# Mask selections ahead of GpSimd's loads, another layout for k and q of two pairs, another order of the front, and one set of loads less

## The chip, the cores and the metric

The kernel runs on one core of a Trainium2 chip. The metric is the device time of one execution in microseconds. TensorE (PE) multiplies matrices, VectorE (DVE) and ScalarE (ACT) work elementwise, GpSimd (POOL) makes masks and zeroes and also issues some DMAs, and SyncE (SP) issues the others.

## The reference

Four batches of 8 heads, 576 positions, head dimension 64, all in float32. Attention first, in two parts that are added; then two gated feed-forward blocks, the first on the attention's output, the second on the first's.

```python
def attention(q, k, v):
    # pooled part: means of 4 neighbouring positions, softmax over 144, repeated 4 times
    q_d, k_d, v_d = (t.reshape(B, H, S // 4, 4, D).mean(axis=3) for t in (q, k, v))
    out_up = np.repeat(sm_attn(q_d, k_d, v_d), 4, axis=2)
    # local part: only keys with |i - j| < 4
    scores = scale * np.matmul(q, k.transpose(0, 1, 3, 2))
    scores = np.where(mask, scores, -1e9)
    return out_up + softmax(scores) @ v

def moe(x, w_in, conv_w, w_out):        # 512 -> 1024 -> 512
    h = np.maximum(x @ w_in, 0.0)
    gate = sigmoid(conv over 3 positions of h, one filter per channel)
    return (h * gate) @ w_out

def moe2(x, w_val, conv_w, w_out):      # 512 -> 512 -> 512
    gate = sigmoid(causal conv over 5 positions of x)
    return (gate * (x @ w_val)) @ w_out
```

## The kernel before

**Units of work.** A step `s` is one pair of heads of one batch: pairs 0 to 3 are batch 0, pair 4 is the first of batch 1, 16 in all. For each pair: k and q are loaded with positions on partitions and transposed on PE (`tpk`, `tpq`, in `transp`), evacuated by ACT (`kT`, `qT`, in `evac`), pooled by DVE (`kd`, `qd`); v is pooled (`pv`). The local part works on 24 blocks of 24 queries against 32 keys: `sl` adds the mask by a matmul of identity and `maskr` and then the scores, `mxl`, `sub`, `xl`, `sml`, `mul` are the softmax, `tr` transposes, `avl` and `avm` multiply with the windows of v (tile `ldw`), `xn` and `xo` add the pooled part. The pooled part is `sd`, `mxd`, `xd`, `smd`, `scd`, `etd`, `etc`, `avd`, `od`. The pair's output is split into two numbers of lower precision (`xhi`, `xlo`) for the first feed-forward block, whose matmuls run as three products of high and low parts.

**Weights.** They come as raw 64-bit words; each block of 128 x 512 is converted and split by `Weights.pieces`: `ab` (ACT), `cv` (four DVE instructions), `hi` (ACT), `lo` (one DVE instruction). There are 8 blocks for w_in and 8 for w_out (two for each of the four column blocks of the second matmul).

**The front.** Batch 0's attention is written out by hand as the list `FRONT`: names of steps with the pair's number, issued in that order on PE, DVE and ACT, each engine in order (`ordered`). The first four w_in splits (`ab0` to `lo3`) and the convolution weights (`cwa0` to `cwc0`) are in it too. Ahead of it, SP is handed the loads in this order: k and q of pairs 0 and 1, v of the first four heads, half of the windows of v (12 gathers), k and q of pair 2, the rest of v, k and q of pair 3, four blocks of w_in, the convolution weights, and v, k, q of pair 4. POOL makes the identity, zeroes the two tiles `h`, makes `mask` (a zeroing and 12 selections, two for each of six regions) and issues the other 12 gathers; in which order these stand on POOL is left to the scheduler. In batch 0, k and q lie with a partition's six positions of one head side by side (`[QT, 2, NT, D]`), and each transpose takes 12 matmuls; in later batches the two heads lie side by side (`[QT, NT, 2, D]`), and it takes 6 in transpose mode. Each matmul of the 12 is two records in the profile.

**The rest.** From pair 4 on each pair takes eight slots, and between slots PE gets units of the feed-forward block of the batch before: 16 units of the first matmul (`a_mm`, two for each of 8 column blocks, behind each pair of which DVE runs the convolution over 3 positions and the gate) and 16 of the second (`b_mm`, four for each of 4 column blocks). `due_at(slot)` tells how many units must have been issued by a slot. In batch 0 a unit whose index is in `SPLITS` also splits a weight block and loads a further one; the first four of them are w_in's, the other eight w_out's. `next_load` and `next_v` load k, q, v of the pair after; they also ran at pair 3 and so loaded pair 4's again, which had been loaded ahead of the stream.

Of the kernel before, what the change touches and what calls it, by code (L numbers as in the profile page):

```python
# [8 lines left out]
F32 = mybir.dt.float32  # L9
# [54 lines left out]
def kernel(  # L64
# [13 lines left out]
    nc = tc.nc  # L78
    B, H, S, D = q.shape
# [4 lines left out]
    HP = H // 2  # L84
    SD = S // 4
    HD = SD // 2
    QT = 96
    NT = S // QT
# [14 lines left out]
    NSTEP = B * HP  # L103
# [3 lines left out]
    mp = ctx.enter_context(tc.tile_pool(name="mp", bufs=1))  # L107
# [5 lines left out]
    mask = const.tile([128, MW], F32, name="mask")  # L113
# [6 lines left out]
    HT = [mp.tile([128, S + 2], F32, name=f"h{i}") for i in range(2)]  # L120
    turn = {"n": 0, "both": True}

    def pair(name):

        turn["n"] += 1
        pool = psm if turn["both"] and turn["n"] % 2 else psd
        return pool.tile([128, 2, 512], F32, tag="pair", name=name)
# [6 lines left out]
    def key_start(j):  # L134

        return min(max(QB * j - 4, 0), S - KB)
# [3 lines left out]
    def mm(*a, **kw):  # L140
        last["pe"] = nc.tensor.matmul(*a, **kw)  # L141
# [12 lines left out]
            return call  # L154

    vec, act = Noted(nc.vector, "vec"), Noted(nc.scalar, "act")

    def ordered(fn, engines=("pe",)):

        with ExitStack() as st:  # L160
            for e in engines:
                if e in last:
                    st.enter_context(tc.issue_after(last[e].ins))
            fn()

    def beneath(fn):

        was = dict(last)
        ordered(fn, ("pe", "vec", "act"))
        last.update(was)  # L170
# [20 lines left out]
    class Weights:  # L191
# [8 lines left out]
        def load(self, queue=nc.gpsimd):  # L200
            if not self.jobs:
                return
            dst, src, r0, nr, c0 = self.jobs.pop(0)
            wide = PW // nr
            rows = src[r0 * 128 : (r0 + nr) * 128]
            t, w = self.stage(self.n)
            self.n += 1
            if src.dtype == F32:
                queue.dma_start(
                    out=w.rearrange("p (r n) -> p r n", r=nr),  # L210
                    in_=rows.rearrange("(r p) n -> p r n", p=128)[:, :, c0 : c0 + wide],
                )
            else:
                queue.dma_start(
                    out=t.rearrange("p (r n) -> p r n", r=nr),
                    in_=rows.bitcast(I32).rearrange("(r p) n -> p r n", p=128)[
                        :, :, 2 * c0 : 2 * (c0 + wide)
                    ],
                )
            self.staged.append((t, w, src.dtype == F32, dst, r0, nr, c0))  # L220
# [22 lines left out]
    T, Y = {}, {}  # L243

    def load_v(b, hp):
        t = ap.tile([HD, 2, 2, 4, D], F32, tag="ldv", name="ldv", bufs=1)
        nc.sync.dma_start(
            out=t.rearrange("p e s r d -> p e s (r d)"),
            in_=v[b, 2 * hp : 2 * hp + 2].rearrange("h (s p r) d -> p h s (r d)", s=2, r=4),
        )  # L250
        T["ldv", b, hp] = t
# [3 lines left out]
    def load(src, tag, b, hp):  # L255

        if b == 0:
            slot = f"hg{'hi' if tag == 'ldk' else 'lo'}{hp}"
            t = mp.tile([QT, 2, NT, D], F32, tag=slot, name=tag)
            nc.sync.dma_start(  # L260
                out=t.rearrange("p e t d -> p e (t d)"),
                in_=src[b, 2 * hp : 2 * hp + 2].rearrange("h (p t) d -> p h (t d)", p=QT),
            )
        else:
            t = ap.tile([QT, NT, 2, D], F32, tag=tag, name=tag, bufs=1)
            for e in range(2):
                nc.sync.dma_start(
                    out=t[:, :, e, :], in_=src[b, 2 * hp + e].rearrange("(t p) d -> p t d", p=QT)
                )
        T[tag, b, hp] = t  # L270
# [14 lines left out]
    def load_vw_first(queue, blocks):  # L285

        if "w" not in first:
            first["w"] = keep.tile([128, NG, H, D], F32, tag="wout0", name="ldw")
        vw = first["w"]
        for g in range(NG):  # L290
            for c in blocks:
                k0 = key_start(c * NG + g)
                queue.dma_start(
                    out=vw[KB * c : KB * c + KB, g], in_=v[0, :, k0 : k0 + KB].rearrange("h k d -> k h d")
                )
        for hp in range(HP):
            T["ldw", 0, hp] = vw[:, :, 2 * hp : 2 * hp + 2]
# [32 lines left out]
    def transp(s, name):  # L330
        src = T.pop(("ld" + name, *where(s)))
        p = pair("tp")
        inrow = src.shape[1] == 2
        for i in range(NT):
            to = p[:, i // 3, i % 3 * QT : i % 3 * QT + QT]
            if inrow:
                for e in range(2):
                    mm(to[ROWS[e]], src[:, e, i], ident[:QT, :QT], start=True, stop=True)
            else:
                mm(to, src[:, i].rearrange("p e d -> p (e d)"), ident[:QT, :QT], is_transpose=True)  # L340
        T["tp" + name, s] = p, inrow

    def evac(s, name):
        p, inrow = T.pop(("tp" + name, s))
        t = ap.tile([128, S], F32, tag=name + "T", name=name + "T", bufs=1)
        if inrow:
            to = t.rearrange("c (p s i) -> c p s i", s=2, i=3)
            pv = p[:, :, : 3 * QT].rearrange("c s (i p) -> c p s i", i=3)
        else:
            to, pv = t.rearrange("c (s p) -> c s p", s=2), p[:, :, : 3 * QT]  # L350
        act.activation(out=to, in_=pv, func=AF.Copy, scale={"k": scale, "q": 1.0}[name])
        T[name + "T", s] = t
# [202 lines left out]
    def where(s):  # L555
        return s // HP, s % HP
# [30 lines left out]
    XO = []  # L587

    def next_load(s, name):
        if HP <= s + 1 < NSTEP:  # L590
            load({"k": k, "q": q}[name], "ld" + name, *where(s + 1))

    def next_v(s):
        if HP <= s + 1 < NSTEP:
            load_v(*where(s + 1))

    def prep(s, name):
        transp(s, name)
        evac(s, name)
        pooled(s, name)  # L600
        next_load(s, name)
# [35 lines left out]
    def split_x(b, kk, x):  # L637
        parts(x, [XH[:, kk], xl(b)[:, kk]])
# [186 lines left out]
    for hp in range(2):  # L825
        load(k, "ldk", 0, hp)
        load(q, "ldq", 0, hp)
    load_v_first(0)
    load_vw_first(nc.sync, (0, 1))
    for h in HT:  # L830
        nc.gpsimd.memset(h, 0.0)
    nc.gpsimd.memset(mask, 0.0)
    m3 = mask[:, : NG * KB].rearrange("p (g k) -> p g k", k=KB)
    spans = [(c, 0, NG, 4) for c in range(4)]
    spans[0] = (0, 1, NG - 1, 4)
# [1 line left out]
    for c, g, n, off in spans + [(0, 0, 1, 0), (3, NG - 1, 1, QB * (NB - 1) - key_start(NB - 1))]:  # L837
        m = m3[32 * c : 32 * c + 32, g : g + n]
        for sgn in (1, -1):
            nc.gpsimd.affine_select(  # L840
                out=m,
                in_=m,
                compare_op=ALU.is_ge,
                fill=BIG,
                base=3 - sgn * off,
                pattern=[[0, n], [sgn, KB]],
                channel_multiplier=-sgn,
            )
    vec.tensor_copy(identr, ident)
    vec.tensor_copy(maskr, mask)  # L850
    load_vw_first(nc.gpsimd, (2, 3))

    def stage(n):
        tag = ("y1", "y2", "y3", "g")[n % 4] if n < 9 else ("y2", "y3", "g")[n % 3]
# [19 lines left out]
    for src, o, m in ((conv3, 0, 3 * KF), (conv5, 3 * KF, 5 * KM)):  # L874
        if src.dtype == F32:
            nc.sync.dma_start(out=cwf[o : o + m], in_=src.rearrange("t (f p) -> (t f) p", p=128))
        else:
            nc.sync.dma_start(
                out=cw[o : o + m, :256], in_=src.bitcast(I32).rearrange("t (f p) -> (t f) p", p=256)
# [15 lines left out]
    def due_at(n):  # L895

        n -= 4
        if n > 80:
            return n - (n - 80) // 2
        if n > 32:  # L900
            return n
        n += 4
        return n * 16 // 14 if n < 14 else 16 + (n - 14) * 16 // 22

    def step_unit():

# [6 lines left out]
        for x in ready:  # L913
            XO.remove(x)
            split_x(*x)
        if b == 0 and m in SPLITS:
            beneath(lambda: (W.split(), W.load()))
# [10 lines left out]
                behind(conv5_e, 1, e)  # L928

    ALL = ("pe", "vec", "act")  # L930
    SPLITS = (0, 2, 4, 6, 8, 10, 12, 14, 16, 18, 20, 22)
    FRONT = """
        tpk0 tpq0 kT0 kd0 qT0 pv0 sl0 qd0 pv1 sd0 mxl0 tpq1 mxd0 sub0 xd0 tpk1 qT1 smd0 scd0 qd1
        kT1 etd0 xl0 kd1 sl1 sml0 etc0 mul0 tr0 sd1 mxl1 sub1 avd0 mxd1 xl1 sml1 xd1 tpq2 mul1 pv2
        od0 avl0 qT2 smd1 scd1 qd2 avm0 xn0 tpk2 xo0 tr1 xhi0 xlo0 etd1 kT2 kd2 sl2 etc1 ab0 cv0
        sd2 avd1 mxd2 hi0 tpq3 ab1 mxl2 xd2 sub2 lo0 pv3 od1 tpk3 qT3 xl2 smd2 qd3 ab2 scd2 sml2
        avl1 mul2 kT3 etd2 xn1 kd3 ab3 avm1 cv1 etc2 sd3 xo1 hi1 sl3 mxd3 xhi1 tr2 xd3 xlo1 avd2
        mxl3 cwa0 smd3 tpk4 od2 sub3 scd3 cv3 avl2 xl3 kT4 avm2 xn2 hi3 etd3 sml3 xo2 tpq4 etc3
        mul3 xhi2 tr3 avd3 cv2 qT4 od3 avl3 cwv0 hi2 avm3 xn3 xlo2 cwp0 xo3 cwc0 xhi3 lo3 xlo3 lo2
        lo1 pv4 qd4 kd4  # L940
    """.split()

    def by_name():
# [54 lines left out]
    slot = 0  # L998
# [77 lines left out]
```

## Time and profile before

| | us |
|---|---|
| median of 3 runs | 495.88 |
| lowest, highest | 494.71, 499.05 |
| profiled execution, device time | 497.79 |
| its span (first to last instruction) | 496.0 |
| PE busy | 449.8 (91%) |
| DVE busy | 362.0 (73%) |
| ACT busy | 266.4 (54%) |
| POOL busy | 22.1 (4%) |

The profile is of one execution. Busy time counts compute instructions; a matmul's end is modelled, so a busy PE need not be at its peak. [...] In a timeline, a line is an instruction or a merged row of equal ones with its count; in brackets stands how long its engine was idle before it and what released it; "issue" there means that the profile shows nothing that it waited for.

### The profile page before, as it was taken

How to read it: one execution, taken by the hardware profiler on the slowest of the kernel's cores; microseconds unless marked ns; L12 is line 12 of the kernel's file. 1: busy time of each engine (PE TensorE's matmuls, PEld its weight loads, DVE VectorE, ACT ScalarE, POOL GpSimd, SP SyncE). 2: the span in 40 equal slices, each digit the busy share in tenths (PEclk: the TensorE clock that was granted, in tenths of full speed). 3: DMA queues.
4: the chain of work that ended last, by engine and by line, in shares of the span. 5: the costliest groups of instructions: out<-in, count | busy, mean ns of one | idle time of the engine just before them, and what ended most of it. 6: DMA issues, size and time to landing. Idle time of an engine off the chain costs nothing.

```text
span 496.0 us, 13820 instructions
## 1 busy us (share of the span) xinstructions
PE 449.8 (91%) x5961; PEld 415.2 (84%) x5961; DVE 362.0 (73%) x655; ACT 266.4 (54%) x564; POOL 22.1 (4%) x49
## 2 busy tenths in 40 slices
PE   3669995987798999999999999999979999999997
PEld 3469885976698998987999988899979999889985
DVE  0588998999976458898857998338999775939530
ACT  2357637677554356784654976426684443635221
POOL 7200010101100000000000000000000000000000
PEclk9985558878777999999999999999999999999999
DMA  9994443424341431413314121142101000210102
GB/s 192 204 256 121 84 155 93 130 64 111 113 123 29 97 78 32 104 29 78 79 35 100 36 48 34 34 166 91 44 1 44 0 1 21 86 65 22 65 23 106
DMA packets 69620, 39.59 MB, mean 80 GB/s; under 512 B 55978, under 2 KB 64502, under 8 KB 69558
## 3 DMA queue, kind: packets, MB, share of 16 engines
q1 hardware_dynamic: 67446, 31.62, 25.3%
q0 software_dynamic: 2112, 7.08, 4.6%
q8 instruction: 47, 0.77, 0.6%
q14 instruction: 15, 0.12, 0.1%
HBM read 33.96 MB, written 4.72 MB: 78 GB/s over the span
## 4 chain that ended last, share of the span: by engine, by line
PE 58%; DVE 23%; ACT 9%; DMA 5%; issue 4%; POOL 1%; POOLq 0%; DVEq 0%; ACTq 0%
PE pb L141 20%; PE pc L141 10%; PE pd L141 10%; DVE cv L151 8%; PE pa L141 7%; PE avl L141 4%; DMA ldv<-in_v_dram 3%; DVE stage L151 3%; PE tp L141 2%; DVE hglo L151 2%; ACT ed L151 2%; ACT cv L151 2%; ACT h L151 2%; DMA ldw<-in_v_dram 2%; PE sl L141 1%
## 5 line engine op out<-in xcount | busy, mean ns | idle before, releaser
L141 PE MATMUL pb<-hghi,wout 128*128 128x288 f32 x512 | 105.6, 316 | 3.9 <-ACT hghi L151 3.9
L141 PE MATMUL pa<-xhi,win 128*128 128x288 f32 x512 | 104.4, 313 | 0.0
L141 PEld LDWEIGHTS pb<-hghi,wout 128*128 128x128 f32 x512 | 81.7, 200 | 7.1 <-ACT hghi L151 4.4
L141 PEld LDWEIGHTS pa<-xhi,win 128*128 128x128 f32 x512 | 80.2, 197 | 3.0 <-issue 2.3
L141 PE MATMUL pb<-hglo,wout 128*128 128x288 f32 x256 | 57.6, 307 | 0.5 <-DVE hglo L151 0.5
L141 PE MATMUL pa<-xlo,win 128*128 128x288 f32 x256 | 56.6, 304 | 0.0
L151 DVE SCALAR_TENSOR_TENSOR cv<-h,cwt,cv 128x576 f32<-128x576 f32 x64 | 51.3, 810 | 5.4 <-ACT cv L151 5.1
L141 PEld LDWEIGHTS pc<-ys,wval 128*128 128x128 f32 x384 | 51.6, 188 | 0.6
L141 PE MATMUL pc<-ys,wval 128*128 128x288 f32 x384 | 52.0, 294 | 0.0
L151 DVE SCALAR_TENSOR_TENSOR g<-y,cwt,g 128x576 f32<-128x576 f32 x64 | 49.8, 810 | 0.3
L141 PEld LDWEIGHTS avl<-et,ldw 32*64 32x64 f32 x1536 | 31.0, 164 | 20.1 <-issue 14.1
L141 PE MATMUL avl<-et,ldw 32*64 32x24 f32 x1536 | 34.0, 237 | 13.9 <-issue 8.4
L141 PE MATMUL pd<-wout,hghi 128*128 128x512 f32 x144 | 45.3, 395 | 0.0
L141 PEld LDWEIGHTS pb<-hglo,wout 128*128 128x128 f32 x256 | 43.7, 200 | 1.0 <-DVE hglo L151 1.0
L141 PEld LDWEIGHTS pa<-xlo,win 128*128 128x128 f32 x256 | 43.2, 198 | 0.0
L151 ACT ACTIVATE ed<-sd,mxd 72x144 f32<-72x144 f32 x64 | 23.2, 370 | 21.1 <-DVE mxd L151 21.0
L141 PEld LDWEIGHTS pd<-wout,hghi 128*128 128x128 f32 x144 | 26.8, 188 | 5.9
L151 ACT ACTIVATE cv<-cv 128x576 f32<-128x576 f32 x32 | 21.9, 683 | 15.5 <-DVE cv L151 15.2
L151 ACT ACTIVATE hghi<-gvf 128x576 fp32r<-128x576 f32 x16 | 11.0, 686 | 34.0 <-DVE gvf L151 34.0
L141 PE MATMUL pd<-wout,hglo 128*128 128x512 f32 x72 | 28.0, 395 | 0.0
L151 DVE SCALAR_TENSOR_TENSOR cv<-cv,h 128x576 f32<-128x576 f32 x32 | 23.8, 749 | 4.6 <-ACT cv L151 4.4
L151 DVE SCALAR_TENSOR_TENSOR gvf<-g,pc 128x576 f32<-128x576 f32 x16 | 11.9, 752 | 20.5 <-PE pc L141 20.5
(90 smaller groups left out, 712.9 us busy)
## 6 DMA issues: line engine op xcount, KB each, us to landing
out_dram<-o SPq DMA_DIRECT2D x18, 256.0 KB
stage<-in_moe_w_out_dram POOLq DMA_DIRECT2D x8, 512.0 KB, 3.8
ldv<-in_v_dram SPq DMA_DIRECT2D x13, 288.0 KB
ldk<-in_k_dram SPq DMA_DIRECT2D x26, 144.0 KB
ldq<-in_q_dram SPq DMA_DIRECT2D x26, 144.0 KB
ldw<-in_v_dram SPq DMA_DIRECT2D x48, 48.0 KB
stage<-in_moe_w_in_dram SPq DMA_DIRECT2D x4, 512.0 KB
stage<-in_moe_w_in_dram POOLq DMA_DIRECT2D x4, 512.0 KB, 5.9
```

Source lines behind the costliest of these rows:

```text
L141: last["pe"] = nc.tensor.matmul(*a, **kw)
L151: last[self.key] = getattr(self.engine, name)(*a, **kw)
```

## The change

POOL's mask is zeroed first, and an order is pinned: identity, mask, and behind the mask's last selection six gathers (window block 3) and the zeroing of `h`. SP gets 18 gathers (blocks 0, 1, 2) in place of 12. k and q of pairs 2 and 3 of batch 0 are loaded head beside head, by two DMAs each; `transp` takes the short form for them, while `evac` still undoes the order of positions for every pair of batch 0. `next_load` and `next_v` no longer run for pair 4. The `SPLITS` of w_out stand at units 11 to 25 and not at 8 to 22; by `due_at` batch 0's first 16 units are issued within 12 slots and not 14, and the next 16 within 24 and not 22. `FRONT` has another order.

```diff
--- before.py
+++ after.py
@@ -154,6 +154,7 @@
             return call
 
     vec, act = Noted(nc.vector, "vec"), Noted(nc.scalar, "act")
+    pool = Noted(nc.gpsimd, "pool")
 
     def ordered(fn, engines=("pe",)):
 
@@ -256,11 +257,18 @@
 
         if b == 0:
             slot = f"hg{'hi' if tag == 'ldk' else 'lo'}{hp}"
-            t = mp.tile([QT, 2, NT, D], F32, tag=slot, name=tag)
-            nc.sync.dma_start(
-                out=t.rearrange("p e t d -> p e (t d)"),
-                in_=src[b, 2 * hp : 2 * hp + 2].rearrange("h (p t) d -> p h (t d)", p=QT),
-            )
+            if hp < 2:
+                t = mp.tile([QT, 2, NT, D], F32, tag=slot, name=tag)
+                nc.sync.dma_start(
+                    out=t.rearrange("p e t d -> p e (t d)"),
+                    in_=src[b, 2 * hp : 2 * hp + 2].rearrange("h (p t) d -> p h (t d)", p=QT),
+                )
+            else:
+                t = mp.tile([QT, NT, 2, D], F32, tag=slot, name=tag)
+                for e in range(2):
+                    nc.sync.dma_start(
+                        out=t[:, :, e, :], in_=src[b, 2 * hp + e].rearrange("(p t) d -> p t d", p=QT)
+                    )
         else:
             t = ap.tile([QT, NT, 2, D], F32, tag=tag, name=tag, bufs=1)
             for e in range(2):
@@ -330,20 +338,19 @@
     def transp(s, name):
         src = T.pop(("ld" + name, *where(s)))
         p = pair("tp")
-        inrow = src.shape[1] == 2
         for i in range(NT):
             to = p[:, i // 3, i % 3 * QT : i % 3 * QT + QT]
-            if inrow:
+            if src.shape[1] == 2:
                 for e in range(2):
                     mm(to[ROWS[e]], src[:, e, i], ident[:QT, :QT], start=True, stop=True)
             else:
                 mm(to, src[:, i].rearrange("p e d -> p (e d)"), ident[:QT, :QT], is_transpose=True)
-        T["tp" + name, s] = p, inrow
+        T["tp" + name, s] = p
 
     def evac(s, name):
-        p, inrow = T.pop(("tp" + name, s))
+        p = T.pop(("tp" + name, s))
         t = ap.tile([128, S], F32, tag=name + "T", name=name + "T", bufs=1)
-        if inrow:
+        if s < HP:
             to = t.rearrange("c (p s i) -> c p s i", s=2, i=3)
             pv = p[:, :, : 3 * QT].rearrange("c s (i p) -> c p s i", i=3)
         else:
@@ -587,11 +594,11 @@
     XO = []
 
     def next_load(s, name):
-        if HP <= s + 1 < NSTEP:
+        if HP < s + 1 < NSTEP:
             load({"k": k, "q": q}[name], "ld" + name, *where(s + 1))
 
     def next_v(s):
-        if HP <= s + 1 < NSTEP:
+        if HP < s + 1 < NSTEP:
             load_v(*where(s + 1))
 
     def prep(s, name):
@@ -826,10 +833,8 @@
         load(k, "ldk", 0, hp)
         load(q, "ldq", 0, hp)
     load_v_first(0)
-    load_vw_first(nc.sync, (0, 1))
-    for h in HT:
-        nc.gpsimd.memset(h, 0.0)
-    nc.gpsimd.memset(mask, 0.0)
+    load_vw_first(nc.sync, (0, 1, 2))
+    pool.memset(mask, 0.0)
     m3 = mask[:, : NG * KB].rearrange("p (g k) -> p g k", k=KB)
     spans = [(c, 0, NG, 4) for c in range(4)]
     spans[0] = (0, 1, NG - 1, 4)
@@ -837,7 +842,7 @@
     for c, g, n, off in spans + [(0, 0, 1, 0), (3, NG - 1, 1, QB * (NB - 1) - key_start(NB - 1))]:
         m = m3[32 * c : 32 * c + 32, g : g + n]
         for sgn in (1, -1):
-            nc.gpsimd.affine_select(
+            pool.affine_select(
                 out=m,
                 in_=m,
                 compare_op=ALU.is_ge,
@@ -848,7 +853,13 @@
             )
     vec.tensor_copy(identr, ident)
     vec.tensor_copy(maskr, mask)
-    load_vw_first(nc.gpsimd, (2, 3))
+
+    def behind_masks():
+        load_vw_first(nc.gpsimd, (3,))
+        for h in HT:
+            nc.gpsimd.memset(h, 0.0)
+
+    ordered(behind_masks, ("pool",))
 
     def stage(n):
         tag = ("y1", "y2", "y3", "g")[n % 4] if n < 9 else ("y2", "y3", "g")[n % 3]
@@ -900,7 +911,7 @@
         if n > 32:
             return n
         n += 4
-        return n * 16 // 14 if n < 14 else 16 + (n - 14) * 16 // 22
+        return n * 16 // 12 if n < 12 else 16 + (n - 12) * 16 // 24
 
     def step_unit():
 
@@ -928,16 +939,16 @@
                 behind(conv5_e, 1, e)
 
     ALL = ("pe", "vec", "act")
-    SPLITS = (0, 2, 4, 6, 8, 10, 12, 14, 16, 18, 20, 22)
+    SPLITS = (0, 2, 4, 6, 11, 13, 15, 17, 19, 21, 23, 25)
     FRONT = """
-        tpk0 tpq0 kT0 kd0 qT0 pv0 sl0 qd0 pv1 sd0 mxl0 tpq1 mxd0 sub0 xd0 tpk1 qT1 smd0 scd0 qd1
-        kT1 etd0 xl0 kd1 sl1 sml0 etc0 mul0 tr0 sd1 mxl1 sub1 avd0 mxd1 xl1 sml1 xd1 tpq2 mul1 pv2
-        od0 avl0 qT2 smd1 scd1 qd2 avm0 xn0 tpk2 xo0 tr1 xhi0 xlo0 etd1 kT2 kd2 sl2 etc1 ab0 cv0
-        sd2 avd1 mxd2 hi0 tpq3 ab1 mxl2 xd2 sub2 lo0 pv3 od1 tpk3 qT3 xl2 smd2 qd3 ab2 scd2 sml2
-        avl1 mul2 kT3 etd2 xn1 kd3 ab3 avm1 cv1 etc2 sd3 xo1 hi1 sl3 mxd3 xhi1 tr2 xd3 xlo1 avd2
-        mxl3 cwa0 smd3 tpk4 od2 sub3 scd3 cv3 avl2 xl3 kT4 avm2 xn2 hi3 etd3 sml3 xo2 tpq4 etc3
-        mul3 xhi2 tr3 avd3 cv2 qT4 od3 avl3 cwv0 hi2 avm3 xn3 xlo2 cwp0 xo3 cwc0 xhi3 lo3 xlo3 lo2
-        lo1 pv4 qd4 kd4
+        tpk0 tpq0 kT0 kd0 qT0 qd0 sl0 sd0 mxl0 sub0 tpq1 mxd0 xl0 sml0 xd0 mul0 tpk1 tr0 qT1 smd0
+        qd1 scd0 pv0 kT1 etd0 pv1 sl1 kd1 etc0 avd0 mxl1 sub1 sd1 od0 xl1 sml1 avl0 mxd1 avm0 xn0
+        xd1 mul1 xo0 tpk2 tr1 xhi0 smd1 xlo0 scd1 tpq2 kT2 etd1 qT2 kd2 sl2 qd2 etc1 pv2 sd2 mxl2
+        sub2 avd1 mxd2 xl2 sml2 xd2 tpq3 mul2 tpk3 pv3 od1 qT3 avl1 kT3 smd2 qd3 scd2 avm1 kd3 ab0
+        xn1 etd2 xo1 ab3 tr2 xhi1 cv0 sd3 etc2 ab2 avd2 mxd3 hi0 sl3 od2 xlo1 xd3 lo0 avl2 mxl3
+        ab1 smd3 cwa0 sub3 avm2 scd3 xn2 cv1 tpq4 xl3 etd3 qT4 xo2 hi1 sml3 tpk4 xhi2 etc3 mul3
+        kT4 xlo2 avd3 tr3 cv2 od3 avl3 avm3 cv3 hi2 xn3 hi3 xo3 cwv0 xhi3 xlo3 cwp0 lo2 lo1 lo3
+        cwc0 qd4 kd4 pv4
     """.split()
 
     def by_name():
```

## Rows read from the trace of the kernel before

**Rows 1.** Busy time by stretch: us, then each engine; clock, DMA share, GB/s.

```profile
0.00:16.00 16.00, 4.11 (x48) 3.84 (x48) 0.33 (x2) 2.58 (x3) 12.64 (x33) 1.00 0.96 189
16.00:40.00 24.00, 18.76 (x530) 16.30 (x532) 18.00 (x40) 11.51 (x35) 0.00 (x0) 0.84 0.95 218
40.00:70.00 30.00, 28.48 (x614) 24.79 (x614) 28.66 (x64) 16.67 (x46) 3.02 (x4) 0.50 0.44 104
...
80.00:135.00 55.00, 40.59 (x563) 37.26 (x562) 54.33 (x107) 35.71 (x76) 5.00 (x8) 0.81 0.35 101
135.00:175.00 40.00, 38.49 (x609) 35.71 (x607) 24.96 (x54) 17.91 (x47) 0.35 (x1) 0.83 0.32 79
175.00:496.00 321.00, 309.33 (x3535) 287.68 (x3534) 227.91 (x378) 174.15 (x341) 0.34 (x3) 0.99 0.20 55
```

**Rows 2.** Waits of DVE, 0 to 140 us: total, times, longest.

```profile
DVE maskr L151 <- POOL mask L840: 13.0, 1, 13.0
```

**Rows 3.** Chain that ended last, 0 to 50 us: start, duration, what.

```profile
0.88 1.10 POOL h L831 x2
...
3.27 8.16 DMA ldw<-in_v_dram
...
13.72 0.34 POOL mask L840
...
15.90 0.29 DVE maskr L151
16.19 0.66 DVE kd L151
...
28.39 3.90 issue
32.29 2.39 PE avl L141 x96
```

**Rows 4.** Timeline, 0 to 30 us, of several engines: start, duration, engine, instruction.

```profile
3.16 12.75 SPq L293 DMA_DIRECT2D ldw<-in_v_dram  x12
...
6.37 0.65 ACT L151 ACTIVATE kT<-tp 128x576 f32<-128x576 f32 x1 [4.35 <-PE tp L141]
6.73 2.17 POOL L840 TENSOR_SCALAR_AFFINE_SELECT mask<-mask 32x160 f32<-32x160 f32 x6
8.29 0.65 ACT L151 ACTIVATE qT<-tp 128x576 f32<-128x576 f32 x1 [1.27 <-PE tp L141]
```

**Rows 5.** Timeline of PE, transposes of 24 and of 6 records.

```profile
19.79 2.19 PE L141 MATMUL tp<-ident,ldq 96*64 96x96 f32 x24
...
27.20 1.16 PE L141 MATMUL tp<-ident,ldq 96*64 96x96 f32 x24
...
54.28 1.22 PE L141 MATMUL tp<-ident,ldk 96*128 96x96 f32 x6 [0.45 <-DVE smd L151]
```

**Rows 6.** DMA over 0 to 18; SP's queue over 2 to 8, 55 to 64, 10 to 16 us.

```profile
DMA packets 5031, 3.38 MB, mean 188 GB/s; under 512 B 3459, under 2 KB 4839, under 8 KB 5031
...
q1 hardware_dynamic: 1190, 1.45, 98.1%
...
q1 hardware_dynamic: 2368, 0.59, 29.4%
...
q1 hardware_dynamic: 2040, 0.57, 65.8%
```

**Rows 7.** Timeline, 65 to 122 us: first w_in matmul, a w_out split, first w_out matmul.

```profile
65.39 0.85 PE L141 MATMUL pa<-xhi,win 128*128 128x288 f32 x2
...
113.51 0.41 DVE L151 TENSOR_SCALAR stage<-stage 128x512 f32<-128x512 f32 x1
...
113.84 0.68 DVE L151 SCALAR_TENSOR_TENSOR stage<-stage 128x512 int32<-128x512 int32 x1
...
116.71 0.68 DVE L151 TENSOR_TENSOR wout<-stage,wout 128x512 fp32r<-128x512 f32 x1
...
121.64 0.85 PE L141 MATMUL pb<-hghi,wout 128*128 128x288 f32 x2
```

## Prediction

> **What bounds the kernel now.** The first view is the table of stretches [rows 1]. Read the busy columns against each stretch's length. From 0 to 16 us VectorE (DVE) does 0.33 us and TensorE (PE) 4.11: nobody works, though the DMA engines are 0.96 full. From 16 to 40 DVE is busy 18.0 of 24 and PE 18.8. [...] From 80 to 135 DVE is full (54.3 of 55) and PE is not (40.6). From 135 on PE is full (38.5 of 40, then 309 of 321). So the end is set by DVE up to about 135 us and by PE from there; a microsecond that DVE gains before 135 reaches the end, because the PE work behind it then starts earlier, and nothing later hangs on an absolute time.
>
> The second view says why DVE sleeps at first: of all its waits up to 140 us the longest is one of 13.0 us, for the mask [rows 2]. The third, the chain that ended last, gives the reason [rows 3]: GpSimd (POOL) zeroes h, issues gathers of v's windows (ldw), then sits until one of its own gathers has landed (8.16 us), and only then makes the last mask selections, from 13.72 on. maskr is cast at 15.90, and DVE, which runs in order, takes kd0 at 16.19. kT had been there since 7.02 and qT since 8.94 (start plus duration, [rows 4]). The last selections stand on no data from outside.
>
> **The change, part by part.**
>
> *Mask first.* POOL's work ahead of the mask shrinks to identity, mask zeroing and 12 selections. Six of them took 2.17 us [rows 4], so twelve take 4.3; with h's 1.1 us moved behind [rows 3] they can begin near 1.6 and end near 6. That is before kT (7.02). DVE then takes kd0 at about 7.05 in place of 16.19: **-9.1 us** for everything that DVE does behind it, if nothing else is late.
>
> *What is late next.* First, qT: kd0 ends at 7.7, qd0 must wait to 8.94, so 1.2 us of the gain is idle again at once. Second, the dependent steps of pairs 0 and 1 (scores, maximum, exponential, sum) which had 24 us with 6.0 idle on DVE [rows 1]; the new order brings pair 0's chain ahead of pv0 and pv1, which leaves DVE with less to fill that chain's gaps, while the four w_in splits (ab, cv, hi, lo) come later, where they fill others. I put these holes at 0.3 us more than before, with bounds of 3 us less (the stall of the next part gone) and 3 us more. Sum: -9.1 + 1.2 + 0.3 = **-7.6**.
>
> *The stall at avl0.* PE stood 3.90 us before avl0 for nothing that the profile shows [rows 3]. The other engines worked on, and it cost DVE some gaps only from 32 to 40. Whether it comes again is unknown: 0 taken, -3 to 0 (inside the bounds above).
>
> *SP issues 18 gathers, POOL 6.* SP took 12.75 us for 12 [rows 4], 1.06 each, since its queue was full, not because an issue needs that. Ahead of k2 stand the same bytes as before in total (3.38 MB had moved by 18 us, [rows 6]), only on another queue. If DMA engines set the pace, k2 is issued at 16 to 18, as now; if SP's 1.06 holds for each, 18 gathers end at 3.16 + 19.1 = 22.3. Because the engines were 0.96 full [rows 1] I take 17. k2 and q2 (0.59 MB) at the 218 GB/s of 16 to 40 us need 2.7 us, so they are in near 20 to 21; by the moved order tpk2 is wanted near 22. It just fits: 0 in the sum, up to +5 at the far bound. POOL's six gathers follow the mask from 6 to 10 us and block nobody but the zeroing of h, which is wanted after 60.
>
> *Head beside head in pairs 2 and 3.* Four tensors come in eight DMAs with pieces of 256 B in place of four with 1536 B. Of small pieces, 2368 packets took 29.4% of 16 engines for 9 us, 17.9 ns each; of the larger, 1190 took 98.1% for 6 us, 79 ns each for 1218 B [rows 6]. 1.18 MB is 4608 packets x 17.9 / 16 = 5.2 us against 4.8: +0.4 us of a full DMA. In the crowd of 10 to 16 us small ones took 31 ns, which would be 8.9 us: +4.1. Taken: +0.4, hidden if k2 is in time. [...] The trace shows a loss of a tenth per byte, no more.
>
> On PE the four transposes shrink from 24 matmul records to 6: 2.19 to 1.22 us at the lower clock [rows 5], -3.9 us in all. DVE covers it (28.7 of 30), so 0 in the sum, -2 at the far bound; it is also the reserve against PE's lower clock.
>
> *One load of the second batch's first k, q, v less.* Five DMAs, 0.86 MB; they delayed no reader that the rows show (pair 4's first transpose is at 54.28, [rows 5], and its wait is for DVE). 0, at most -1.
>
> *Later w_out splits, another pace.* By slots the first four w_out splits move 0 or 1 slot later, the last four 2 or 3, while the 16 first-phase units of batch 0 end at slot 12 and not 14. A split costs DVE 0.41 x 2 + 0.68 x 2 + 0.68 = 2.9 us [rows 7]. About one split leaves the stretch where DVE is full for the one after 135, where DVE has 15 of 40 us free [rows 1]; the earlier units put the same convolution work a little forward. **-2**, bounds -5 and +1.
>
> Sum: -7.6 - 2 = -9.6. The profiled run took 497.79 us, with a span of 496.0 and 1.8 around it; the median of three runs is 495.88. The same difference gives 488.2 for a run like the profiled one and **486.3** for the median.
>
> **Rivals.**
>
> *DMA sets the front.* If k2, q2 and the second half of v are issued at 22 and not at 17, tpk2 slips by about 4 us and the later ones with it: gain 9.6 - 4 to 6, so 490 to 492. For it: the DMA engines are 0.95 full until 40 us [rows 1] and SP's queue is longer. Against: the bytes are the same and POOL no longer competes early. Chance 0.16.
>
> *PE's lower clock sets the front.* [...] If it stays low throughout, the some 9.5 us of PE work of 20 to 33 us take 19; less the 3.9 saved, 5.6 more, into a PE that had about as much idle time. Gain 9.6 - 4 to 5, so 490 to 491.5. Chance 0.10. [...]
>
> *More than the sum.* If the stall at avl0 goes and PE's 14 idle us of 80 to 135 shrink with the moved splits, -14 to -18: 478 to 482. Chance 0.11.
>
> *Nothing comes of it.* If the mask's selections still wait (POOL's order stays as it was), only the pace is left: 494 to 497. Against it: each edit pins that order. Chance 0.05.
>
> *Slower.* The moved w_out splits miss their readers. The second split ended at 117.4 and the first matmul on w_out began at 121.64 [rows 7]. Three units later, at 3.5 us each (16 units in the 56 us from 65.4, [rows 7]), that split ends near 128; it is wanted two parts into the block, near 133. From a further slip of 5 us on, each of the four column blocks makes PE wait one split: ScalarE 0.7, DVE 2.9, ScalarE 0.6, 4.2 us, 16.7 for four. Without the -2 that is 495.9 - 7.6 + 16.7 = 505. For it: DVE is full just there. Against: the blocks leave room. Chance 0.06.
>
> **How the numbers follow.** The forecast (482.5 to 489.5) has 0.52. Faster by over 1% means under 490.9; 1% is about what a measurement of this kernel can tell, its three runs lying 0.9% apart. Under it: 0.52, 0.11 and half of the 0.26 of the two front rivals, 0.76. Within 1%: the other half and the 0.05, with 0.01 for a partly missed split, 0.18. Slower: 0.06. The range 478.5 to 493 holds the forecast, both front rivals with the late-DMA bound, and most of the better case; it leaves out some 0.15.
>
> **What would show it.** maskr at 6 to 7 us and kd0 at about 7.05; DVE under 3 us of idle time between 9 and 20; POOL's six gathers behind the last selection; sub1 (28.4 now) near 20; k2's issue on SP at 16 to 18 and tpk2 without a DMA wait; DVE full from about 31; the first w_in matmul (65.4 now) near 57; the stretch in which DVE is full ending near 125. Wrong would make it: tpk2 or avl0 waiting for DMA, the transposes at 2.19 us beyond 22 us with PE full, PE waiting for the w_out tiles, or a gap in PE late in the run that is not in the trace of before.

## The result, and the profile after

| | before | after |
|---|---|---|
| median | 497.39 (20 runs, 491.14 to 502.57) | 490.69 (20 runs, 485.88 to 493.06) |
| ratio of paired runs, 95% interval | | 0.9892 [0.9866, 0.9917] |
| profiled execution, span | 497.79, 496.0 | 490.9, 489.1 |
| maskr, kd0 (DVE) | 15.90, 16.19 | 5.84, 6.89 |
| first matmul on w_in, batch 0 (PE) | 65.39 | 60.99 |
| first matmul on w_in, batch 1 (PE) | 177.98 | 169.62 |

The ratio on 497.4 us is -5.4 us (4.1 to 6.7): faster, by a little over half of the 9.6 forecast. The medians alone differ by 6.7, the two profiled executions by 6.9. An execution over 1.5% above the fastest of its kernel is left out of a ratio, as two with the mask alone, the profiled one among them, and one with half the gathers on POOL. The last two rows cut the profiled run into stages: the front became 4.4 us shorter, batch 0's feed-forward block went from 112.6 to 108.6, and the rest from 318.0 to 319.5.

The table of stretches, changed kernel (columns as in [rows 1], the clock as a share of full; the last three rows are finer cuts):

```profile
0.00:16.00 16.00, 11.26 (x207) 9.75 (x207) 7.80 (x18) 6.54 (x18) 9.21 (x27) 1.00 0.96 183
16.00:40.00 24.00, 18.98 (x471) 16.01 (x471) 18.97 (x43) 12.48 (x38) 0.00 (x0) 0.59 0.89 209
40.00:70.00 30.00, 23.48 (x483) 20.99 (x484) 24.22 (x52) 15.53 (x42) 3.01 (x4) 0.59 0.47 125
80.00:135.00 55.00, 41.95 (x594) 38.22 (x593) 51.68 (x100) 33.24 (x73) 5.22 (x8) 0.76 0.33 97
...
6.89:60.99 54.10, 41.80 (x1072) 35.26 (x1068) 43.77 (x96) 29.15 (x82) 4.74 (x9) 0.62 0.73 157
...
15.00:20.00 5.00, 4.14 (x116) 3.05 (x118) 4.02 (x8) 2.28 (x7) 0.00 (x0) 0.69 0.59 114
...
25.00:30.00 5.00, 5.00 (x122) 4.64 (x123) 2.25 (x4) 2.91 (x7) 0.00 (x0) 0.50 1.01 199
```

The same cut of the kernel before, from its kd0 to its first matmul on w_in:

```profile
16.19:65.39 49.20, 43.70 (x1127) 37.88 (x1127) 41.90 (x96) 28.18 (x81) 0.78 (x1) 0.66 0.68 155
```

DVE now works 7.8 us in the first 16 and not 0.3 [rows 1]. But from kd0 to the first matmul on w_in the front takes 54.10 us and not 49.20: DVE is busy 1.9 us more there (w_in's splits have moved ahead of that matmul) and idle 10.3 us and not 7.3. So of the 4.9 us 1.9 are work done earlier, and 3.0 are idle time. The forecast had DVE full from 31; from 40 to 70 it is busy 24.2 of 30, before 28.7.

Timeline of DVE, changed kernel:

```profile
5.84 0.29 DVE L151 CAST maskr<-mask 128x256 fp32r<-128x256 f32 x1 [3.89 <-POOL mask L151]
6.89 0.75 DVE L151 TENSOR_REDUCE kd<-kT 128x144 f32<-128x576 f32 x1 [0.76 <-ACT kT L151]
...
19.26 0.56 DVE L151 TENSOR_TENSOR el<-sl,mxl 128x384 f32<-128x384 f32 x1
...
29.68 0.69 DVE L151 TENSOR_TENSOR ldv<-ldv 72x512 f32<-72x512 f32 x1 [1.24 <-DMA ldv<-in_v_dram]
...
94.01 0.69 DVE L151 TENSOR_TENSOR ldv<-ldv 72x512 f32<-72x512 f32 x1 [2.39 <-DMA ldv<-in_v_dram]
...
98.02 0.55 DVE L151 TENSOR_TENSOR el<-sl,mxl 128x384 f32<-128x384 f32 x1
```

Of the lead of 9.3 us at kd0, 9.1 still stand at pair 1's subtraction, 19.26 against this line of the kernel before:

```profile
28.37 0.56 DVE L151 TENSOR_TENSOR el<-sl,mxl 128x384 f32<-128x384 f32 x1
```

What eats it comes behind that. SP's queue, changed kernel, and its four w_in blocks before:

```profile
3.17 16.67 SPq L301 DMA_DIRECT2D ldw<-in_v_dram  x18
19.89 1.35 SPq L269 DMA_DIRECT2D ldk<-in_k_dram  x2
...
28.46 2.69 SPq L215 DMA_DIRECT2D stage<-in_moe_w_in_dram  x4
```

```profile
19.43 7.14 SPq L214 DMA_DIRECT2D stage<-in_moe_w_in_dram  x4
```

SP hands out k2 at 19.89, not 17. Its 16.67 us are 0.93 for each of 18 gathers, but that merged row holds waits: single gathers took 0.31 to 1.30 us, 0.46 in the median, and 5.2 us lie between them. SP's own waits up to 40 us, changed kernel:

```profile
SPq L301 <- DMA ldv<-in_v_dram: 2.0, 1, 2.0
SPq L301 <- DMA ldw<-in_v_dram: 2.0, 3, 1.3
```

So SP stands for earlier transfers, v's and its own gathers', to land. Only behind the last such wait, which ends at 17.57, does handing out set the pace, while the DMA engines have fallen to 0.59 of full (15 to 20 us). w_in's blocks follow 9 us later than before, v of the next heads 5.7 (22.63 against 16.95). The chain that ended last by 62 us goes through them, changed kernel:

```profile
8.58 8.97 DMA ldw<-in_v_dram
...
17.57 0.31 SPq L301
...
17.92 0.46 SPq L301
...
19.89 0.69 SPq L269
...
28.46 0.84 SPq L215
...
30.65 9.28 DMA stage<-in_moe_w_in_dram
39.95 0.67 ACT stage L151
...
41.19 0.54 ACT etd L151
41.77 1.23 PE avd L141 x8
```

and so does PE's timeline:

```profile
20.88 2.39 PE L141 MATMUL avl<-et,ldw 32*64 32x24 f32 x96
24.80 1.19 PE L141 MATMUL tp<-ident,ldk 96*128 96x96 f32 x6 [1.53 <-ACT xhi L151]
...
41.77 1.23 PE L141 MATMUL avd<-etd,vd 72*64 72x144 f32 x8 [2.64 <-ACT etd L151]
...
48.28 1.22 PE L141 MATMUL tp<-ident,ldq 96*128 96x96 f32 x6
...
58.92 0.30 PE L141 MATMUL cw<-ident,cw 44*128 44x44 f32 x1 [3.51 <-DVE cw L151]
...
60.99 0.85 PE L141 MATMUL pa<-xhi,win 128*128 128x288 f32 x2
...
98.67 1.42 PE L141 MATMUL avl<-et,ldw 32*64 32x24 f32 x48 [4.53 <-issue]
...
118.90 0.55 PE L141 MATMUL pb<-hghi,wout 128*128 128x288 f32 x2 [1.51 <-ACT wout L151]
...
121.51 1.33 PE L141 MATMUL pb<-hghi,wout 128*128 128x288 f32 x4 [1.58 <-DVE wout L151]
```

ACT, in order, waits 2.28 us for a w_in block until 39.95; queued behind that split is the evacuation etd2, and PE's avd2 stands 2.64 us for it. Late loads are also seen in DVE's 1.24 us for v at 29.68; tpk2's wait, which ends at 24.80, is put down to ACT's xhi and not to k2. Just before the first matmul on w_in PE stands 3.51 us for DVE's cw: from 51.31 to there DVE runs almost without a gap (7.30 of 7.61 us) through w_in's splits and the convolution weights. All 14 kernels here with the new `FRONT` show that wait, 3.50 to 3.83 us; the six with the old one show none, or 0.65. It was not tried by itself. In the second matmul PE waits twice for a w_out split (3.1 us together), and 4.53 us at 98.67 under the name "issue".

### The profile page after: what moved, and what is told of

It reads as the page before. It is cut to its first block, busy times and chain, and to the rows that moved or that the text cites. A ratio compares the mean times of both kernels' runs of the same rounds, so it can differ in the third digit from the quotient of the medians.

```text
span 489.1 us, 13679 instructions
## 1 busy us (share of the span) xinstructions
PE 443.3 (91%) x5889; PEld 407.7 (83%) x5889; DVE 362.2 (74%) x655; ACT 265.4 (54%) x564; POOL 18.9 (4%) x43
## 4 chain that ended last, share of the span: by engine, by line
PE 52%; DVE 22%; DMA 10%; ACT 8%; SPq 4%; issue 2%; DVEq 0%; ACTq 0%
PE pb L141 17%; PE pc L141 10%; PE pd L141 10%; DVE cv L151 8%; PE pa L141 6%; DMA ldv<-in_v_dram 4%; PE avl L141 3%; DVE stage L151 2%; DVE hglo L151 2%; DMA stage<-in_moe_w_in_dram 2%; DMA ldw<-in_v_dram 2%; PE tp L141 2%; ACT ed L151 2%; ACT cv L151 2%; ACT h L151 1%
## 5 line engine op out<-in xcount | busy, mean ns | idle before, releaser
L141 PE MATMUL pb<-hghi,wout 128*128 128x288 f32 x512 | 103.6, 311 | 7.0 <-ACT hghi L151 3.9
L141 PEld LDWEIGHTS pb<-hghi,wout 128*128 128x128 f32 x512 | 79.7, 196 | 10.5 <-ACT hghi L151 4.4
L151 DVE SCALAR_TENSOR_TENSOR g<-y,cwt,g 128x576 f32<-128x576 f32 x64 | 49.8, 812 | 0.3
L151 ACT ACTIVATE hghi<-cv 128x576 fp32r<-128x576 f32 x32 | 21.8, 683 | 16.5 <-DVE cv L151 16.3
L151 ACT ACTIVATE cv<-cv 128x576 f32<-128x576 f32 x32 | 21.8, 681 | 12.9 <-DVE cv L151 12.8
```

Source lines behind the costliest of these rows:

```text
L151: last[self.key] = getattr(self.engine, name)(*a, **kw)
```

## The experiments

A ratio is to the kernel before on the same chip, with its 95% interval; 0.001 is 0.5 us. "Front" is the start of batch 0's first matmul on w_in in the profiled execution. Equal fronts come out up to 3.3 us apart (60.99, 61.15, 61.84, 62.35, 64.34 in the five kernels with the changed front), so single fronts less than that apart tell nothing. A difference of two ratios carries both intervals, 1.8 to 3.2 us either way in the pairs below.

**One part alone, one part undone.** The mask alone (order on POOL, 18 and 6 gathers) in the kernel before:

```diff
-    load_vw_first(nc.sync, (0, 1))
+    load_vw_first(nc.sync, (0, 1, 2))
...
-    nc.gpsimd.memset(mask, 0.0)
+    pool.memset(mask, 0.0)
...
-    load_vw_first(nc.gpsimd, (2, 3))
+    ordered(behind_masks, ("pool",))
```

> The kernel before with the mask part alone: mask ahead of GpSimd's loads, 18 gathers on SP and 6 on GpSimd. Theory (the lead of 9 us at the mask is real, and about half is given back because SP hands out k and q of pair 2 four microseconds later): 4 to 7 us faster than before. Rival 1 (the pace change ate the gain of the mask): the mask alone gives 8 to 9 us. Rival 2 (the mask's lead is worth something only with the new order of the front): under 3 us.

0.9898 [0.9853, 0.9943], -5.1 us; front 63.91. Of the four executions behind the ratio three lie at 494.1 to 494.4 and one at 488.94. Of the lead, 8.0 us at pair 0's scores, 4.4 are left at pair 1's: in the old order DVE takes pv0 ahead of qd0, and sd0 needs qd0. That DVE stands there for v's load is the author's reading of that order, not shown by a measured wait.

The changed kernel with that part undone (the same diff, backwards):

> The changed kernel with the mask part undone (GpSimd's order and 12 gathers each as before). Theory: all of the measured gain hangs on the mask, so this is as slow as the kernel before, 0 to 3 us slower even, since its order of the front expects an early mask. Rival 2 (order, layout and pace have a gain of their own): 2 to 4 us faster than before.

0.9949 [0.9922, 0.9975], -2.5 us, 2.8 worse than the whole change; front 65.45: without the mask the front is no shorter than before, and in the profiled execution the block (107.1 us) carries the gain.

The changed kernel with the old pace:

```diff
-SPLITS = (0, 2, 4, 6, 11, 13, ..., 25);  n * 16 // 12 ... 24
+SPLITS = (0, 2, 4, 6, 8, 10, ..., 22);   n * 16 // 14 ... 22
```

> The changed kernel with the old due times and the old units of the w_out splits. By the step of the prediction (-2 for the pace) it is 2 us slower than the changed kernel. Rival 1 (the pace costs: PE waits 3.1 us on w_out, and a v load lands beside two w_out blocks): 2 to 4 us faster than the changed kernel. Theory: within 1 us of it.

0.9908 [0.9877, 0.9938]: 0.8 us worse than the whole change, inside the interval; block 110.2 us against 108.6.

With the old layout for pairs 2 and 3:

```diff
-            if hp < 2:
+            if hp < 4:
```

> The changed kernel with k and q of pairs 2 and 3 loaded and transposed in the old layout. Four issues less on SP and larger pieces, but 3.9 us more of PE at its lower clock. Theory (SP's issues bound this stretch, PE is hidden): 0 to 2 us faster than the changed kernel. Rival (PE at the lower clock bounds the front): 2 to 4 us slower.

0.9936 [0.9911, 0.9961]: 2.2 us worse (0.4 to 4.0); front 63.31. Whatever the large pieces bring is less than what the layout costs, and pair 2's 24-record transposes take 2.19 and 2.17 us there, at a granted clock of 0.50.

With the old `FRONT` (the diff's last block, backwards):

> The changed kernel with the old order of the front. Theory (the front is bound by what SP hands out, and the mask alone already gave 5 us): within 2 us of the changed kernel, so 4 to 8 us faster than before. Rival (the new order is what makes the early mask pay): as slow as before, within 2 us.

0.9900 [0.9862, 0.9939], front 61.34: not told apart from the whole change.

With pair 4's loads made twice again:

```diff
-        if HP < s + 1 < NSTEP:
+        if HP <= s + 1 < NSTEP:
```

> The changed kernel with the second batch's first k, q, v loaded twice again. All theories: within 1.5 us of the changed kernel, since 4 us of DMA time fall where the DMA engines are half idle. Against them all would be a loss of over 2 us.

1.0010 [0.9984, 1.0035]: the whole gain is gone; front 66.93. PE's timeline and SP's queue of this kernel:

```profile
54.25 1.19 PE L141 MATMUL tp<-ident,ldq 96*128 96x96 f32 x6 [6.34 <-DMA ldq<-in_q_dram]
```

```profile
48.20 1.32 SPq L275 DMA_DIRECT2D ldk<-in_k_dram  x2
49.56 7.40 SPq L275 DMA_DIRECT2D ldq<-in_q_dram  x4
```

The new order wants pair 4's q at 48; the second load of it is handed out from 49.56 on, and PE stands 6.34 us.

**SP's queue.** k2 and q2 ahead of the gathers:

```diff
+    load(k, "ldk", 0, 2)
+    load(q, "ldq", 0, 2)
     load_vw_first(nc.sync, (0, 1, 2))
...
-    for hp in range(2, HP):
+    load_v_first(1)
-        load(k, "ldk", 0, hp) ...
+    load(k, "ldk", 0, 3) ...
```

> The changed kernel with k and q of pair 2 handed out by SP ahead of its 18 gathers. Theory (SP's order sets the front: k2 was issued at 19.89 and VectorE then had gaps of 2.75 us from 25 to 30): tpk2 no longer waits for a load, the front gets 2 to 3 us shorter, and the whole 1 to 3 us, if the gathers are still in by the time that avl0 wants them. Rival (the gathers are as urgent): avl0 waits instead, 0 to 3 us slower.

0.9904 [0.9868, 0.9940], front 62.89: no gain; avl0 now waits for the gathers (0.73, 1.41 and 0.59 us).

12 gathers on SP, 12 on POOL, still behind the mask:

```diff
-load_vw_first(nc.sync, (0, 1, 2)) ... load_vw_first(nc.gpsimd, (3,))
+load_vw_first(nc.sync, (0, 1))    ... load_vw_first(nc.gpsimd, (2, 3))
```

> The changed kernel with 12 gathers on SP and 12 on GpSimd, behind the mask. Theory (SP's 16.7 us for 18 gathers hold up k2): k2 is issued at 15 to 17 in place of 19.9, gain 1 to 3 us. Rival (DMA engines, not the queue, set the pace): k2 earlier, but it lands no earlier; within 1 us.

0.9836 [0.9787, 0.9886], -8.2 us, 2.8 beyond the change, which is just the interval of that difference; k2 is handed out at 16.00, front 59.49. The chain of this kernel shows no transfer any more between 23 and 60 us, but up to 48 PE at its lower level (granted clock 0.50 in every stretch from 20 to 61 us), two 6-record transposes in 2.11 us, and from 49.8 DVE:

```profile
23.48 2.11 PE tp L141 x12
...
30.01 1.17 PE sd L141 x8
31.18 1.16 PE avd L141 x8
32.33 2.11 PE tp L141 x12
```

The same split of the gathers, alone in the kernel before:

> The kernel before with the mask ahead of GpSimd's loads alone, and 12 gathers on each queue as before (run e1 had 18 on SP). Theory (SP's six further gathers hold up k and q of pair 2): 1 to 3 us faster than e1, so 6 to 9 us under the kernel before. Rival: same as e1, 5 us under.

0.9935 [0.9904, 0.9967], front 63.9: 1.8 us worse than the mask alone with 18 and 6, within the interval. In the old order no gain from SP's queue is seen.

**VectorE's pooling of v.** Up to 190 us DVE waited 9.3 us in five places for v (before 4.1 in three), as at 29.68 and 94.01 above; over the whole run 12.8 us, before 6.8. Behind the front the scheduler puts that pooling early, and what is behind it on DVE, in order, waits with it (2.39 us at 94.01). From pair 5 on it is pinned behind the DVE instruction ahead of it:

```diff
-put(5, s + 1, ..., pool_v, next_v)
+put(5, s + 1, ..., lambda s: ordered(lambda: pool_v(s), ("pe", "vec")), next_v)
```

> The changed kernel with one thing more: from pair 5 on, VectorE's pooling of a pair's v stands behind the pooling of its q, and no longer earlier in the queue. Theory (the lead is lost after the front because VectorE, in order, stands 9.3 us at v's single buffer in the changed kernel, 4.1 us in the one before, and PE's avl behind it): the waits for v fall under 3 us, PE's 'issue' waits shrink, 2 to 5 us faster than the changed kernel. Rival (those waits have slack behind them): within 1 us.

0.9635 [0.9602, 0.9668], 481.05 us: 12.8 us beyond the change. DVE's wait for v is 1.1 us in the whole run.

The same pin in the kernel before:

> The same pinning in the kernel before, as a control. Theory: it stood only 4.1 us at v, so it gains 0 to 2 us. Rival (the pinning has a worth of its own, which the changed kernel did not lose): as much as in the changed kernel, 2 to 5 us.

0.9746 [0.9713, 0.9780], 487.04 us: 12.7 us here too. So the waits that the change adds are not, as far as the intervals tell, where its gain went; pinned, the change is worth 0.9635 / 0.9746 = 0.989 (0.984 to 0.993), as without. The pin does more than move one step: PE's list of instructions stays the same, but DVE's, and ACT's with it, is another from pair 5 on. Batch 0's block takes 102.0 us and not 112.6 in the kernel before, 101.1 and not 108.6 in the changed one.

**Parts, with the pin.** The parts were weighed again with the pin. Old `SPLITS` (the first line of the pace's diff):

> The changed kernel with v pinned (e9) and the w_out splits at their old units; the due times stay new. Theory (the lead of 9.8 us at pair 5 falls to 6.4 at pair 7 because PE waits 4.1 us for the second half of w_out's first column block): that wait goes, 1.5 to 4 us faster than e9 (481.05). Step of the prediction (later splits relieve VectorE): 1 to 3 us slower than e9. Rival (VectorE is full there, so what PE does not wait for it waits for elsewhere): within 0.7 us.

0.9684 [0.9658, 0.9710], 2.4 us worse than the pinned change, a little over the interval of 2.1. Old `SPLITS` and old `due_at`:

> The same with the old due times too. The prediction's step gives 2 us slower than e9. Theory: the earlier first units are worth something, so slower than e13 by 0.5 to 2 us. Rival (due times don't matter where VectorE is full): as e13.

0.9679 [0.9651, 0.9707], 2.2 us worse, just over the interval. PE's waits for w_out splits, two of some 2.1 us in the pinned change, are real:

```profile
115.38 0.54 PE L141 MATMUL pb<-hghi,wout 128*128 128x288 f32 x2 [2.05 <-ACT wout L151]
...
118.45 1.33 PE L141 MATMUL pb<-hghi,wout 128*128 128x288 f32 x4 [2.14 <-DVE wout L151]
```

but on balance the later splits give more than that. The mask alone, in the pinned kernel before:

> The kernel before with v pinned (e10, 487.0) and the mask part of the change alone. If the mask alone carries the gain (as e1 said, 5.1 us with an interval of 2.9 to 7.3): 5 to 6 us faster than e10. If it needs the new order of the front (its trace showed a lead of 8 us at pair 0 and of 4 at pair 1): 1 to 3 us faster.

0.9717 [0.9692, 0.9742]: 1.4 us better than 0.9746, not told apart from nothing; front 62.05. The lead over the pinned kernel before is 8.6 us at pair 0's scores, 5.1 at pair 1's and 3.8 at pair 5's. Its chain:

```profile
19.41 4.00 DMA ldq<-in_q_dram
23.54 1.23 PE tp L141 x24
24.77 2.48 issue
27.25 1.85 PE avl L141 x93
29.10 2.12 PE tp L141 x24
```

The pinned change with pair 4's loads made twice:

> The changed kernel with v pinned and the second batch's first k, q, v loaded twice again. Theory (the new order wants q of pair 4 at 48 us, and the second load of it, issued at 50 to 57, holds it up: tpq4 waited 6.3 us in e6): 4 to 6 us slower than e9. Rival (of the 5.4 us of e6 most was chance in v's waits): 0 to 2 us slower.

0.9786 [0.9755, 0.9817]: 7.5 us worse than the pinned change; front 65.8.

**Best versions.** Half the gathers and the pin:

> The changed kernel with 12 gathers on GpSimd behind the mask and v pinned: both supposed losses undone. Theory: the parts add up, 8 to 11 us less than before from the front and 2 to 4 us from v: 484 to 487 where the kernel before takes 498. Rival (both mend the same wait): no better than the better one of the two alone.

0.9607 [0.9574, 0.9641], 479.91 us: the lowest ratio of all kernels run here, though 1.4 us from the pin alone is within the interval. Its front is 61.00, and its chain leads through the w_in blocks again.

Two w_in splits moved behind the evacuation that PE waits for, in the pinned change and in the version with half the gathers:

```diff
-xn1 etd2 xo1 ab3 tr2 xhi1 cv0 sd3 etc2 ab2 avd2
+xn1 etd2 xo1 tr2 xhi1 cv0 sd3 etc2 ab3 avd2 ab2
```

> The changed kernel with VectorE's pooling of v pinned, and in the front the splits ab3 and ab2 of w_in moved behind etc2. In the trace with the pin ScalarE waited 2.05 us at 39.53 for a block of w_in, whose load SP had handed out at 28.3 behind 18 gathers and the loads of k and q, and etd2, queued behind it on ScalarE, kept TensorE's avd2 2.41 us. Theory (the late w_in load sets the front, through ScalarE's order): avd2 starts about 2 us earlier without that wait, the first matmul on w_in comes 1 to 2 us before 61.2, and the time falls by 1 to 2 us against the pinned change (ratio about 0.961). Rival (the lower clock of TensorE and VectorE's work hold the front anyway): the wait goes, but the first matmul on w_in stays within 61 to 63, and the ratio within 0.962 to 0.966.

0.9626 [0.9584, 0.9669]. PE of this kernel:

```profile
39.12 1.23 PE L141 MATMUL avd<-etd,vd 72*64 72x144 f32 x8
...
59.70 0.85 PE L141 MATMUL pa<-xhi,win 128*128 128x288 f32 x2
```

avd2 starts 2.2 us earlier than with the pin alone (41.36), without a wait; of that 1.45 reach the first matmul on w_in, and 0.5 of the time, less than its interval.

> The same move of ab3 and ab2 in the best kernel so far (12 gathers on SP, 12 on GpSimd behind the mask, v's pooling pinned; ratio 0.9607, first matmul on w_in at 61.0, where ScalarE waited 1.60 us for the w_in block). Theory: 1 to 1.5 us less, ratio about 0.958, first matmul on w_in near 59.5. Rival: no change, 0.960 to 0.962.

0.9631 [0.9583, 0.9680], front 60.06: no gain. PE's avd2 no longer waits; the chain from 23 us on is PE at the lower level (0.50 from 20 to 61) and, from 50, DVE. Against the run before it, this is the moving of six gathers a third time: 0.9631 for 0.9626, no gain either.

## Why the forecast was too high

**Right.** *Mask first:* kd0 came at 6.89 for 7.05, maskr at 5.84, the selections took 4.28 us for 4.3; the lead held to pair 1's subtraction, 19.26 for "near 20". The stall at avl0, taken as 0, did not come again: avl0 started at 20.88 without a wait.

**The step that failed: "What is late next".** It charged 1.5 us (1.2 for qT, 0.3 for the holes) and let SP's queue cost 0. The runs show DVE idle 3.0 us more between kd0 and the first matmul on w_in, twice the charge: qT's part came as forecast (1.17), the holes were 1.8 and not 0.3. That matmul came at 60.99, where 57 was forecast (57.8 by the step's own -7.6).

The 4.9 us of the lead that are missing there aren't all loss: 1.9 are DVE work done earlier, which the block behind gets back. So counted, an estimate from the one profiled pair, the front gained 6.3 us for 7.6 and the block 2.1 for 2. Behind them "nothing later hangs on an absolute time" put the rest at 0, and it lost 1.5: DVE stood 5.9 us for v in five places there, before 4.4. What is left between the profiled pair's 6.9 and the ratio's 5.4 lies between executions.

The pinned pair reads otherwise. Its front is idle 1.5 us more, the charge itself, and so gained 7.7; the block lost 1.0 where 2 were to be gained, and PE waits 4.2 us for w_out's splits there; the rest differs by 0.1. It is one execution of each, and fronts scatter by 3.3 us, so how much of the shortfall belongs to which step stays open. (In the chances, 0.13 + 0.05 + 0.01 is 0.19 and not 0.18; nothing hangs on it.)

Three things of that step were wrong or left out; what each costs stays open too:
- SP. "SP took 1.06 each since its queue was full, not because an issue needs that" holds as far as it was measured: in the kernel before, SP stood 3.8 of the 12.75 us for transfers to land (v's 2.8, its own gathers' 1.0), while a gather takes 0.45 in the median, and 0.46 in the changed kernel; a full queue is the author's reading of these waits. What failed is the price of 0 and k2 at 17. The queue had the six further gathers to wait for and then to hand out, and k2 went out at 19.89. And the working counted only k2, q2 and v behind the gathers; the four w_in blocks stand in the same queue. They went out 9 us later and landed at 39.9, and ACT's order carried that wait to PE. What this costs in time isn't shown: moving six gathers to POOL brings k2 to 16.00, and the time down by 2.8 us, by 1.4 with the pin, and by nothing in the last pair, none of it clear of its interval; taking w_in's wait away gave 0.5, within it too.
- Behind SP stands PE at its lower level: the granted clock is 0.50 from 20 to 30 and, but for 0.84 from 30 to 35, on to 61, and with SP relieved PE is the chain up to 48. The forecast hid the short transposes' 3.9 us under DVE, at 0 with a far bound of -2; undone they cost 2.2 (0.4 to 4.0), so the bound was nearer than the 0.
- Behind PE stands DVE from 50 on. The w_in splits were to "come later, where they fill others"; the trace shows them in a row ahead of cw, for which PE waits 3.51 us.

The rival "DMA sets the front" named the place, and its time (490 to 492) is the measured one. Its condition, k2 out at 22, was met by half, and since the queue's price isn't shown, that the time agrees may be luck. "PE's lower clock" appears in the chain once SP is relieved, at a granted clock of 0.50. Its doubling of 9.5 us to 19 is an estimate: a 24-record transpose took 1.16 us at 27.20 [rows 5], and 2.19 and 2.17 in the old layout's run at 0.50. In the kernel before PE is busy 8.5 us from 20 to 33, where 9.5 were taken. What the lower level costs by itself no run shows: from 30 to 35 and from 35 to 40 the clock was 0.82 and 0.86 in the old layout's run, 0.84 and 0.50 in the changed kernel, one execution of each.

**Loads once, "0, at most -1":** wrong with the rest of the change in. The reason, that pair 4's transpose at 54.28 waits for DVE, is a row of the old order; in the new one q is wanted at 48.28, and loading twice costs 5.9 us (7.5 pinned). In the trace of before pair 4's q is transposed at 58.72 without a wait; the new order can't hide the second load.

**Pace, -2:** right in size: 2.2 and 2.4 us with the pin, just clear of the interval, 0.8 within it without. The mechanism of the slower rival, PE waiting for w_out splits, appears with 3 to 4 us of waits and is outweighed. Of the unpinned pair's stages (-4.4, -4.0, +1.5) the second and third hold changes of the scheduler's that the pin takes away; pinned they are -5.8, -0.9 and +0.1.

**256-byte pieces, +0.4 hidden:** nothing speaks against it; the large ones came out 2.2 us slower, PE's longer transposes included, so the pieces' own price isn't seen alone; no run here shows a loss from them that outweighs PE's gain.

The prices of the parts don't add up: undone singly in the pinned change, the pace and the second loads alone give 9.7 us, more than the whole 5.5. What stays open is the mask's own share: alone it is worth 5.1 us (interval 2.8 to 7.3) without the pin and 1.4 with it, and the old `FRONT` in the changed kernel was not told apart from the new one. The front read from all runs says the same: 66.2 in the kernel before (with and without the pin), 63.0 with the mask alone (two), 62.1 with the whole change (five).

## What to carry to other kernels

Behind a wait that is removed at the start the next queues come to light: list everything that each in-order queue issues behind the moved instructions, not only the next reader. A merged row of issues hides waits, so price an issue by single ones and by the queue's own waits. A mark in the run also moves when work moves across it: count idle time beside it. "It delays no reader" is read against the new order, since moving readers forward makes a hidden load visible. Try a control for any cure found on the way: the pin that seemed to repair this change was worth as much without it, and more than twice the change itself.

## What the runs showed that was not expected

- Another DVE order in the middle of the run, set off by pinning one small step, took some 12.7 us off either kernel, with PE's list unchanged.
- PE's wait of 4.53 us called "issue" (98.67) ends with DVE's subtraction on the scores (98.02 + 0.55): before it DVE stood 2.39 us for v. The granted clock, 1.00 at 90 to 98 us, was 0.60 from 98 to 102 and 0.50 from 102 to 106: the gap at 94 to 98.6, in which PE was busy 0.14 us, was followed by the lower level. What the profile can't name may be another engine that has yet to give a buffer back; that reading wasn't tried by itself.
- The clock's column can mislead: the pinned kernel before shows 1.00 throughout 40 to 70 us, while a 6-record transpose takes 1.22 us there, as at the lower level [rows 5].
